# A borrowed PSUM bank for the first product of a quad, in a Mamba-2 plus PReLU kernel

## The chip, the cores and the metric

The kernel runs on one core of one Trainium2 chip. The metric is the device time in microseconds (us), the median of several runs; the time before is 369.48 us (three runs, 368.27 to 370.26). A profile of one execution, with a span of 366.2 us, gives the times of single instructions. Engines are named as the profile names them: PE is TensorE (matmuls; PEld are its weight loads), DVE is VectorE, ACT is ScalarE, POOL is GpSimd, SP issues DMAs.

## The reference, cut to what matters

A chunked state-space scan makes `x` of 3072 tokens by 256 features, and a two-layer network with a PReLU follows:

```python
# scan, per batch and head, in chunks of 32 tokens (the kernel uses chunks of 128)
y_intra = einsum('bhij,bhjd->bhid', (C @ B^T) * L, x)      # L: decays, causal
y_inter = einsum('bhin,bhnd->bhid', C, state) * exp(cum)
state   = decay_full * state + sum_j(B_j x_j * decay_from_j)
# network: 3072 tokens, d_model 256, d_ff 2048
h = x @ w_in
g = maximum(h, 0) + alpha * minimum(h, 0)
out = g @ w_out
```

All of it is in float32. The network's two products are most of the arithmetic.

## The kernel before, the parts concerned

**Seven products in place of eight.** Five of the six groups of 512 tokens go through a Strassen-like scheme on 2x2 blocks. A *quad* is a step of this scheme: (group g, z), four blocks of 128 hidden features, two halves of 256 tokens. There are 4 quads (z = 0 to 3) in each of the groups 1 to 5, so 20 in all. In a quad, seven first products (`first`) fill the hidden blocks. Each has two matmuls of 128x256, and each of these matmuls is two records in the trace, so a `first` is four records. Seven second products (`product`) of the quad before are strewn between them; `after(j)` is the place where they, and the scan's work, are slipped in.

```python
def quad(g, z, after):
    b11, b12, b21, b22 = ...            # blocks of x (transposed); t1..t4 their differences
    A, Y = (ps_h.tile([P, GT], F32, name="hp")... for i in range(2))   # the two "hp" banks

    def first(to, w, b, start=False):
        for p in range(2):
            nc.tensor.matmul(to[:, p], w(2 * z + p), b, start=start and p == 0, stop=True, ...)

    first(A, lambda q: wi[:, q, 0, 0], b11, True)          # M1
    m1 = tile_of(wtp, "m1", "wt")
    nc.scalar.copy(out=m1, in_=A)                          # L823: M1 is kept in SBUF
    after(1)
    first(Y, lambda q: s1[:, q], t1, True)
    m5 = tile_of(wtp, "m5", "wt")
    nc.scalar.copy(out=m5, in_=Y)                          # L827
    after(2)
    after(3)
    first(A, lambda q: s2[:, q], t2)                       # accumulates on M1 in A
    u2 = tile_of(wtp, "u2", "wg")
    nc.scalar.copy(out=u2, in_=A)                          # L832
    after(4)
    nc.vector.tensor_tensor(out=Y, in0=Y, in1=u2, op=ALU.add)      # L834
    after(5)
    first(A, lambda q: wi[:, q, 1, 0], t3)
    nc.vector.tensor_tensor(out=c22, in0=A, in1=m5, op=ALU.add)    # L838
    after(6)
    first(Y, lambda q: s4[:, q], b22)
    prelu(g12, Y, z, 0)                                    # ACT L798, then DVE L800
    prelu(g22, c22, z, 1, (nc.scalar,))
    nc.scalar.copy(out=Y, in_=m1)                          # L844: M1 back into a bank
    prelu(g22, c22, z, 1, (nc.vector,))
    after(7)
    after(8)
    nc.gpsimd.tensor_tensor(out=tc_, in0=g22, in1=g12, op=ALU.subtract)   # L849
    first(A, lambda q: wi[:, q, 1, 1], t4)
    prelu(g21, A, z, 1)
    after(9)
    after(10)
    first(Y, lambda q: wi[:, q, 0, 1], b21)                # M1 + this product
    prelu(g11, Y, z, 0)
    for o, x0, x1 in ((ta, g12, g11), (tb, g22, ta), (td, tb, g21)):
        eng.tensor_tensor(out=o, in0=x0, in1=x1, op=ALU.subtract)         # L858
    ...
    after(11) ... after(14)
```

`product(g, z, n)` (its matmuls are L790) multiplies block n with weights of `w_out` and accumulates in one of four banks; n = 1, 2, 3 use g11, g21, g22, and 4, 5, 6, 7 use td, ta, tb, tc_.

**PSUM.** There are two `ss` banks (pool `ps_s`, 2 buffers), two `hp` banks (pool `ps_h`, 2 buffers), and four held ones (`bank(0)` to `bank(3)`). Outside the start of the kernel, `ss_tile()` takes the next `ss` bank in turn.

**The scan of later pairs of chunks** runs beside the quads, as a generator whose stages are called from `after`. A pair takes two quads: its last stages run in an odd quad (z = 1, 3), its decays and its `gram` in the even quad before (z = 0, 2).

```python
def turn_bc(gp):                       # DVE transpose of B and C of the next pair
    ...
def pair(gp):
    ...
    if fine:                           # all pairs beside quads
        for k in range(2):
            for w in range(2):
                half_decays(k, w)      # two DVE scans, L460
                if k == 1 and w == 1:
                    spread_c()         # ACT L551
                    c_decayed()        # POOL L554
                yield
    ...
    # gram: 8 matmuls into 2 ss banks and 2 hp banks (L605), then 4 DVE multiplies (L639)
    ...
    if fine and gp + 1 < NP:
        turn_bc(gp + 1)
    yield
    ys = [ss_tile() for w in range(KC)]            # y: matmuls L662, L670
    ...
```

Each scan reads `abc`, which a DMA brings (two of 512 KB for a pair). Of a pair's four `half_decays`, one was called at `after(14)` of the odd quad before, and the others at `after(1)`, `after(2)` and `after(5)` of the even quad. The gram is at `after(13)` of the even quad.

```python
with_gram = {5: ((1,), (2, (0,))), 7: ((2, (1,)), (3,)), 8: ((5, (0,)),), 11: ((5, (1,)), (7,)),
             13: ((6,),), 14: ((4,),)}          # even quads of groups 1 to 4
without = {3: ((1,),), 5: ((2,),), 7: ((3,),), 8: ((5,),), 9: ((7,),), 13: ((6,),), 14: ((4,),)}
for i in range(NZ * (NG - 1)):
    g, z = divmod(NZ + i, NZ)
    nxt = 2 * g + 2                             # NP = 12: no pair is left in group 5
    ...
    quad(g, z, after)
close(NG - 1)
```

The instruction order on each engine is that of the program.

Of the kernel before, what the change touches and what calls it, by code (L numbers as in the profile page):

```python
# [9 lines left out]
F32 = mybir.dt.float32  # L10
U32 = mybir.dt.uint32
U16 = mybir.dt.uint16
ALU = mybir.AluOpType
# [9 lines left out]
def kernel(  # L23
# [25 lines left out]
    nc = tc.nc  # L49
# [4 lines left out]
    batch, H, S, D = x.shape  # L54
    N = B.shape[-1]
    P = 128
    Q = 128
# [11 lines left out]
    NP = NCH // 2  # L69
# [15 lines left out]
    wtp = ctx.enter_context(tc.tile_pool(name="wtp", bufs=3))  # L85
    lda = ctx.enter_context(tc.tile_pool(name="lda", bufs=3))
    ldx = ctx.enter_context(tc.tile_pool(name="ldx", bufs=3))
    work = ctx.enter_context(tc.tile_pool(name="work", bufs=2))
# [4 lines left out]
    gp = ctx.enter_context(tc.tile_pool(name="gp", bufs=16))  # L93
# [12 lines left out]
    ident_p = []  # L106
    m5_bank = []

    def ss_tile():
        if early[0] is None:  # L110
            return ps_s.tile([P, 512], F32, name="ss")
        early[0] += 1
        i = early[0] % (3 if ident_p else 4)
        return ps_s.tile([P, 512], F32, name="ss") if i < 2 else bank(i)


    loads = {}
# [158 lines left out]
    def keep_warm(to, n, cols=2 * Q):  # L276

        for i in range(n):
# [8 lines left out]
                          in_=ident.unsqueeze(1).to_broadcast([P, H, Q]))  # L287
# [137 lines left out]
        return ps_h.tile([P, GT], F32, name="hp", tag="hp")  # L425

    bcs = {}

    def turn_bc(gp):

        bcs[gp] = work.tile([P, 4, Q], F32, name="bc")
        nc.vector.transpose(
            bcs[gp].rearrange("p (i k) t -> p i (k t)", i=2)
            .rearrange("p i (c b) -> p i b c", b=8),
            loads["p", gp][0][:, 1:].rearrange("p e i (b n) -> p (i b) e n", n=N))

    def pair(gp):

        b, c = divmod(2 * gp, CPB)
        nat, abc, xt, ap = loads["p", gp]  # L440
        last = c + 2 == CPB
        fine = gp >= 2 * GC // 2
        dec = work.tile([P, 2, H, Q], F32, name="dec")
        dv = dec.rearrange("p k h t -> p k (h t)")

        def decays(k):

# [7 lines left out]
                                             initial=0.0, op0=ALU.mult, op1=ALU.add)  # L455

        def half_decays(k, w):
            for i in range(2):
                hs = slice((2 * w + i) * 2 * Q, (2 * w + i + 1) * 2 * Q)
                nc.vector.tensor_tensor_scan(out=dv[:, k, hs], data0=abc[k][:, hs],  # L460
                                             data1=ident_p[0], initial=0.0, op0=ALU.mult,
                                             op1=ALU.add)

        ahead = {}

# [1 line left out]
        if gp == 0:  # L467
            z = first_a(ap, nc.vector)
# [105 lines left out]
        if fine:  # L574
            for k in range(2):
                for w in range(2):
                    half_decays(k, w)
                    if k == 1 and w == 1:
                        spread_c()
                        c_decayed()  # L580
                    yield
        else:
            if gp > 1:
                states(added(ss_tile()))
                c_decayed()
            decays(0)
            if gp == 1:
                dps = added(dps)
            if gp:
                yield  # L590
            if gp != 1:
                decays(1)
            if gp > 1:
                spread_c()
# [199 lines left out]
    def prelu(o, h, z, i, by=(nc.scalar, nc.vector)):  # L794

        fs = [slice(4 * z + 2 * p + i, 4 * z + 2 * p + i + 1) for p in range(2)]
        for p in range(2 if nc.scalar in by else 0):
            nc.scalar.mul(o[:, p], h[:, p], s_alpha[:, fs[p]])  # L798
        for p in range(2 if nc.vector in by else 0):
            nc.vector.scalar_tensor_tensor(out=o[:, p], in0=h[:, p], scalar=s_mul[:, fs[p]],  # L800
                                           in1=o[:, p], op0=ALU.mult, op1=ALU.max)

    def quad(g, z, after):


        b11, b12 = (xts[g][:, 0, h * HT : (h + 1) * HT] for h in range(2))
        b21, b22 = (xts[g][:, 1, h * HT : (h + 1) * HT] for h in range(2))
        t1, t2, t3, t4 = xsums[g]
        s1, s2, s4 = in_sums
        A, Y = (ps_h.tile([P, GT], F32, name="hp").rearrange("p (q t) -> p q t", q=2)  # L810
                for i in range(2))

        def first(to, w, b, start=False):
            for p in range(2):
                nc.tensor.matmul(to[:, p], w(2 * z + p), b, start=start and p == 0, stop=True,  # L815
                                 skip_group_check=True)

        def tile_of(pool, name, tag):
            return pool.tile([P, 2, HT], F32, name=name, tag=tag)

        first(A, lambda q: wi[:, q, 0, 0], b11, True)
        m1 = tile_of(wtp, "m1", "wt")
        nc.scalar.copy(out=m1, in_=A)  # L823
        after(1)
        first(Y, lambda q: s1[:, q], t1, True)
        m5 = tile_of(wtp, "m5", "wt")
# [3 lines that stand above are left out]
        first(A, lambda q: s2[:, q], t2)  # L830
        u2 = tile_of(wtp, "u2", "wg")
        nc.scalar.copy(out=u2, in_=A)  # L832
        after(4)
        nc.vector.tensor_tensor(out=Y, in0=Y, in1=u2, op=ALU.add)  # L834
        after(5)
        first(A, lambda q: wi[:, q, 1, 0], t3)
        c22 = tile_of(wtp, "c22", "wg")
        nc.vector.tensor_tensor(out=c22, in0=A, in1=m5, op=ALU.add)  # L838
        after(6)
        first(Y, lambda q: s4[:, q], b22)  # L840
        g12, g22, g21, g11 = (tile_of(gp, "gt", "gt") for i in range(4))
        prelu(g12, Y, z, 0)
        prelu(g22, c22, z, 1, (nc.scalar,))
        nc.scalar.copy(out=Y, in_=m1)  # L844
        prelu(g22, c22, z, 1, (nc.vector,))
        after(7)
        after(8)
        ta, tb, tc_, td = (tile_of(gp, "gt", "gt") for i in range(4))
        nc.gpsimd.tensor_tensor(out=tc_, in0=g22, in1=g12, op=ALU.subtract)  # L849
        first(A, lambda q: wi[:, q, 1, 1], t4)  # L850
        prelu(g21, A, z, 1)
        after(9)
        after(10)
        first(Y, lambda q: wi[:, q, 0, 1], b21)
        prelu(g11, Y, z, 0)
        for o, x0, x1 in ((ta, g12, g11), (tb, g22, ta), (td, tb, g21)):
            eng = nc.vector if g == NG - 1 and z == NZ - 1 and o is not td else nc.gpsimd
            eng.tensor_tensor(out=o, in0=x0, in1=x1, op=ALU.subtract)  # L858
        blocks[g, z] = {1: g11, 2: g21, 3: g22, 4: td, 5: ta, 6: tb, 7: tc_}
        after(11)  # L860
        after(12)
        after(13)
        after(14)
# [157 lines left out]
    for f in range(FIRST, NF):  # L1021
# [21 lines left out]
        if f in in_steps:  # L1043
# [18 lines left out]
            14: ((2, 1), (3, 1))}  # L1062


    with_gram = {5: ((1,), (2, (0,))), 7: ((2, (1,)), (3,)), 8: ((5, (0,)),), 11: ((5, (1,)), (7,)),
                 13: ((6,),), 14: ((4,),)}
    without = {3: ((1,),), 5: ((2,),), 7: ((3,),), 8: ((5,),), 9: ((7,),), 13: ((6,),), 14: ((4,),)}
    for i in range(NZ * (NG - 1)):
        g, z = divmod(NZ + i, NZ)
        nxt = 2 * g + 2  # L1070

        def after(j, g=g, z=z, i=i, nxt=nxt):
            places = with_gram if nxt < NP and z % 2 == 0 else without
            for n in places.get(j, ()) if i else ():
                product(*divmod(NZ + i - 1, NZ), *n)
            if i == 0:
                for f, half in last_out.get(j, ()):
                    output(NF - LATE + f, half)
            if (i, j) in ((0, 13), (1, 2)):
                store_first(i)  # L1080
            for args in late_sums.get((i, j), ()):
                weight_sums(*args)
            if g > 1 and z == 0 and j in (7, 11, 13, 14):
                if j == 7:
                    comb[0] = combine(g - 1)
                next(comb[0], None)
            if g > 1 and z in (1, 3) and j == 11:
                finish(g - 1, z // 2)
            if nxt + steps.get((z, j), NP) < NP:
                ssm(nxt + steps[z, j])  # L1090

                if j == 5 and z % 2:
                    for p in (1, 0, 1):
                        if nxt + z // 2 + p < NP:
                            ssm(nxt + z // 2 + p)
            if nxt < NP and (z, j) == (3, 7):
                token_sums(g + 1)
            ahead = nxt + {(0, 9): 1, (2, 9): 2}.get((z, j), NP)
            if ahead < NP:
                if ahead == 6:  # L1100
                    rows_turn(1, held["pr"])
                bns[ahead] = pair_loads(ahead)

        comb = [None] if i == 0 else comb
        if z == 0 and nxt < NP:
            load_pair(nxt + 1)
        if z == 2 and nxt + 2 < NP:
            load_pair(nxt + 2)
        quad(g, z, after)
    close(NG - 1)  # L1110


# [28 lines left out]
```

## Time and profile before

| | |
|---|---|
| median time | 369.48 us |
| span of the profiled execution | 366.2 us |
| busy, PE / PEld | 359.1 / 287.8 us |
| busy, DVE / ACT / POOL | 253.1 / 175.6 / 201.7 us |
| granted TensorE clock | 1.00 |
| quads begin / end on PE (first matmul of L815 to the last product) | 81.7 us / 361.5 us |

Read the busy times as shares of the span: only PE is near all of it. But a matmul's time in the trace overlaps the next one's, so a busy PE may still be held up. What tells is the distance between the starts of matmuls that follow each other.

### The profile page before, as it was taken

What the parts mean: (1) busy time and instruction counts of PE and PEld (TensorE: products, weight loads), DVE (VectorE), ACT (ScalarE), POOL (GpSimd) and SP (SyncE); (2) the same over time, 40 slices, a digit from 0 to 9 for tenths busy, and PEclk for the clock granted to TensorE, in tenths of its full rate; (3) what the DMA queues carried; (4) which work ended last, traced back from release to release, by engine and by line L of the source; (5) the groups of instructions that cost most, each with busy time, mean ns of one, the idle gap of its engine ahead of it and who ended that gap; (6) DMA issues with size and microseconds to landing.
All of it is one profiled execution on the core that took longest, in us unless ns stands there. A gap on an engine that the chain in (4) does not pass through costs nothing.

```text
span 366.2 us, 6758 instructions
## 1 busy us (share of the span) xinstructions
PE 359.1 (98%) x2515; PEld 287.8 (79%) x2515; DVE 253.1 (69%) x469; ACT 175.6 (48%) x377; POOL 201.7 (55%) x211
## 2 busy tenths in 40 slices
PE   8989999999999999999999999999999999999996
PEld 8766666568888888788788788788788788888884
DVE  7897999968648848848748858658858634643364
ACT  1657956426355345444444544445445434544441
POOL 4876666779938855725635626537436345254512
PEclk9999999999999999999999999999999999999999
DMA  7989998822075302004503603701711001001004
GB/s 147 199 180 345 239 284 187 178 61 57 30 167 108 100 3 59 0 2 75 154 3 66 163 5 57 173 2 32 166 37 29 2 2 29 1 2 29 0 0 89
DMA packets 111017, 31.68 MB, mean 87 GB/s; under 512 B 79288, under 2 KB 106888, under 8 KB 110984
## 3 DMA queue, kind: packets, MB, share of 16 engines
q1 hardware_dynamic: 105872, 30.66, 35.5%
q10 hardware_dynamic: 5112, 0.59, 1.1%
q8 instruction: 20, 0.33, 0.4%
q14 instruction: 13, 0.11, 0.1%
HBM read 27.89 MB, written 3.34 MB: 85 GB/s over the span
## 4 chain that ended last, share of the span: by engine, by line
PE 83%; DVE 8%; DMA 4%; POOL 2%; issue 1%; ACT 1%; ACTq 0%; POOLq 0%; SPq 0%; DVEq 0%
PE hp L815 35%; PE bank L790 33%; PE bank L729 4%; PE ss L670 3%; DVE dec L460 3%; PE hp L691 2%; PE ss L605 2%; DMA rows<-in_a_dram 2%; PE ss L662 1%; DVE wr L248 1%; DMA nat<-in_B_dram 1%; PE hp L706 1%; DMA raw<-in_moe_w_in_dram 1%; DVE gt L695 1%; DVE wr L247 1%
## 5 line engine op out<-in xcount | busy, mean ns | idle before, releaser
L858 POOL TENSOR_TENSOR gt<-gt 128x512 f32<-128x512 f32 x58 | 73.6, 1270 | 37.4 <-DVE gt L800 30.7
L790 PE MATMUL bank<-gt,w_out 128*128 128x256 f32 x320 | 82.4, 381 | 0.0
L800 DVE SCALAR_TENSOR_TENSOR gt<-hp,s_mul,gt 128x256 f32<-128x256 f32 x120 | 52.4, 479 | 42.3 <-ACT gt L798 40.2
L798 ACT ACTIVATE gt<-hp,s_alpha 128x256 f32<-128x256 f32 x120 | 50.3, 470 | 50.1 <-PE hp L815 42.7
L790 PEld LDWEIGHTS bank<-gt,w_out 128*128 128x128 f32 x320 | 60.1, 190 | 10.4 <-issue 2.3
L790 PE MATMUL bank<-gt,ws 128*128 128x256 f32 x240 | 59.5, 379 | 0.0
L849 POOL TENSOR_TENSOR gt<-gt 128x512 f32<-128x512 f32 x20 | 25.4, 1270 | 56.0 <-DVE gt L800 56.0
L790 PEld LDWEIGHTS bank<-gt,ws 128*128 128x128 f32 x240 | 45.6, 190 | 6.2
L460 DVE TENSOR_TENSOR_SCAN dec<-abc,bank 128x256 f32<-128x256 f32 x80 | 48.0, 659 | 0.0
L815 PE MATMUL hp<-xs,w_in 128*128 128x256 f32 x160 | 42.3, 387 | 0.0
L815 PE MATMUL hp<-xT,w_in 128*128 128x256 f32 x160 | 41.9, 384 | 0.1
L815 PE MATMUL hp<-xs,ws 128*128 128x256 f32 x160 | 40.7, 382 | 0.0
L823 ACT COPY m<-hp 128x512 f32<-128x512 f32 x20 | 11.7, 586 | 52.9 <-PE hp L815 48.1
L815 PEld LDWEIGHTS hp<-xT,w_in 128*128 128x128 f32 x160 | 29.2, 190 | 7.1 <-ACT hp L844 2.9
L815 PEld LDWEIGHTS hp<-xs,ws 128*128 128x128 f32 x160 | 29.8, 190 | 5.5 <-POOL gt L858 1.1
L815 PEld LDWEIGHTS hp<-xs,w_in 128*128 128x128 f32 x160 | 29.3, 190 | 5.6 <-ACT u L832 0.6
L834 DVE TENSOR_TENSOR hp<-hp,u 128x512 f32<-128x512 f32 x20 | 13.8, 690 | 27.3 <-ACT u L832 27.3
L729 PE MATMUL bank<-w_out,gt 128*128 128x256 f32 x128 | 31.0, 384 | 0.0
L729 PEld LDWEIGHTS bank<-w_out,gt 128*128 128x128 f32 x128 | 23.7, 190 | 6.4 <-issue 3.3
L513 POOL TENSOR_TENSOR sm<-state,bmask 128x256 f32<-128x256 f32 (+1 forms) x12 | 7.9, 656 | 31.8 <-DVE state L510 31.7
L691 PE MATMUL hp<-xT,w_in 128*128 128x512 f32 x48 | 22.8, 597 | 0.4 <-DVE gt L718 0.2
L800 DVE SCALAR_TENSOR_TENSOR gt<-c,s_mul,gt 128x256 f32<-128x256 f32 x40 | 21.3, 573 | 0.0
(157 smaller groups left out, 542.5 us busy)
## 6 DMA issues: line engine op xcount, KB each, us to landing
abc<-z SPq DMA_DIRECT2D x20, 512.0 KB
raw<-in_moe_w_in_dram SPq DMA_DIRECT2D x8, 512.0 KB
raw<-in_moe_w_out_dram SPq DMA_DIRECT2D x8, 512.0 KB
xt<-in_x_dram SPq DMA_DIRECT2D x24, 128.0 KB
nat<-in_B_dram SPq DMA_DIRECT2D x36, 64.0 KB
out_dram<-o_sb SPq DMA_DIRECT2D x32, 64.0 KB
nat<-in_C_dram SPq DMA_DIRECT2D x22, 64.0 KB
ap<-pf SPq DMA_DIRECT2D x11, 128.0 KB
```

Source lines behind the costliest of these rows:

```text
L460: nc.vector.tensor_tensor_scan(out=dv[:, k, hs], data0=abc[k][:, hs], data1=ident_p[0], initial=0.0, op0=ALU.mult, op1=ALU.add)
L670: nc.tensor.matmul(y[w][32 * q : 32 * q + 32, k], xt[:, k, h * D : (h + 1) * D], dec[:, k, h], start=False, stop=True, tile_position=(0, 3 ...
L691: nc.tensor.matmul(hp, w_in[:, k, f * P : (f + 1) * P], xts[g][:, k], start=(k == 0), stop=(k == KC - 1))
L729: nc.tensor.matmul(pos[0][t // 2][:, t % 2], gt[:, t * Q : (t + 1) * Q], w_out[:, f], start=(f == 0 and t % 2 == 0), stop=(f == NF - 1), s ...
L790: nc.tensor.matmul(ms[g][i][:, h], w, blocks[g, z][n][:, p], start=(q == 0 and h == 0), stop=(q == NQ - 1), skip_group_check=True)
L798: nc.scalar.mul(o[:, p], h[:, p], s_alpha[:, fs[p]])
L800: nc.vector.scalar_tensor_tensor(out=o[:, p], in0=h[:, p], scalar=s_mul[:, fs[p]], in1=o[:, p], op0=ALU.mult, op1=ALU.max)
L815: nc.tensor.matmul(to[:, p], w(2 * z + p), b, start=start and p == 0, stop=True, skip_group_check=True)
L823: nc.scalar.copy(out=m1, in_=A)
L834: nc.vector.tensor_tensor(out=Y, in0=Y, in1=u2, op=ALU.add)
L849: nc.gpsimd.tensor_tensor(out=tc_, in0=g22, in1=g12, op=ALU.subtract)
L858: eng.tensor_tensor(out=o, in0=x0, in1=x1, op=ALU.subtract)
```

## The change: what it does and what it is for

In 12 of the 20 quads (the even ones of groups 1 to 4, and all four of the last group; `third` is true there) the first product M1 is made in an `ss` bank, Z, in place of A. ACT then copies Z into A, and Z itself stays as it is. So M1 needs no copy in SBUF and no copy back into Y, and the product that is added to it for g11 can be made early, at `after(5)`, in Z. In even quads the second products stand in another order (`with_gram`): half of product 1 comes at `after(3)`, between the copy of Z and the product that needs it, and products 3 and 5 at `after(9)`. The first two scans of a pair are moved from `after(14)` of an odd quad to `after(1)` of that odd quad, right behind the transposes of `turn_bc`; the other stages move up accordingly, so that an even quad has two scans fewer in front of L834. All this is meant to take waits of PE for ACT and DVE out of the even quads.

```diff
+    decs = {}
+    def scan_half(dec, abc, k, w):          # the body of half_decays, moved out
+        ...
     def turn_bc(gp):
         ...
+        decs[gp] = work.tile([P, 2, H, Q], F32, name="dec")
+        scan_half(decs[gp], loads["p", gp][1], 0, 0)
@@ pair
-        dec = work.tile([P, 2, H, Q], F32, name="dec")
+        dec = decs.pop(gp) if gp in decs else work.tile([P, 2, H, Q], F32, name="dec")
+        begun_scans = gp in bcs
@@ pair, if fine
-                    half_decays(k, w)
+                    if begun_scans and (k, w) != (1, 1):
+                        if (k, w) != (1, 0):
+                            half_decays(*divmod(2 * k + w + 1, 2))
+                    else:
+                        half_decays(k, w)
@@ quad
-    def quad(g, z, after):
+    def quad(g, z, after, third):
...
-        first(A, lambda q: wi[:, q, 0, 0], b11, True)
-        m1 = tile_of(wtp, "m1", "wt")
-        nc.scalar.copy(out=m1, in_=A)
+        if third:
+            Z = ss_tile().rearrange("p (q t) -> p q t", q=2)
+            first(Z, lambda q: wi[:, q, 0, 0], b11, True)
+            nc.scalar.copy(out=A, in_=Z)
+        else:
+            (as before)
...
         nc.vector.tensor_tensor(out=Y, in0=Y, in1=u2, op=ALU.add)
+        g12, g22, g21, g11 = (tile_of(gp, "gt", "gt") for i in range(4))
+        if third:
+            first(Z, lambda q: wi[:, q, 0, 1], b21)
+            prelu(g11, Z, z, 0, (nc.scalar,))
         after(5)
         first(A, lambda q: wi[:, q, 1, 0], t3)
         nc.vector.tensor_tensor(out=c22, in0=A, in1=m5, op=ALU.add)
+        if third:
+            prelu(g11, Z, z, 0, (nc.vector,))
         after(6)
...
-        nc.scalar.copy(out=Y, in_=m1)
+        if not third:
+            nc.scalar.copy(out=Y, in_=m1)
...
-        first(Y, lambda q: wi[:, q, 0, 1], b21)
-        prelu(g11, Y, z, 0)
+        if not third:
+            first(Y, lambda q: wi[:, q, 0, 1], b21)
+            prelu(g11, Y, z, 0)
@@ the order of second products
-    with_gram = {5: ((1,), (2, (0,))), 7: ((2, (1,)), (3,)), 8: ((5, (0,)),), 11: ((5, (1,)), (7,)),
-                 13: ((6,),), 14: ((4,),)}
+    with_gram = {3: ((1, (0,)),), 5: ((1, (1,)), (2, (0,))), 7: ((2, (1,)), (3, (0,))),
+                 9: ((3, (1,)), (5,)), 11: ((7,),), 13: ((6,),), 14: ((4,),)}
...
-        quad(g, z, after)
+        quad(g, z, after, nxt >= NP or z % 2 == 0)
```

More of the change, by code (lines that the diff above doesn't have):

```diff
@@ L427 @@
     bcs = {}
+    decs = {}
+    def scan_half(dec, abc, k, w):
+        dv = dec.rearrange("p k h t -> p k (h t)")
+        for i in range(2):
+            hs = slice((2 * w + i) * 2 * Q, (2 * w + i + 1) * 2 * Q)
+            nc.vector.tensor_tensor_scan(out=dv[:, k, hs], data0=abc[k][:, hs],
+                                         data1=ident_p[0], initial=0.0, op0=ALU.mult,
+                                         op1=ALU.add)
     def turn_bc(gp):
@@ L457, in half_decays @@
         def half_decays(k, w):
[L458 to L462, printed above, removed]
+            scan_half(dec, abc, k, w)
         ahead = {}
@@ L819, in tile_of @@
             return pool.tile([P, 2, HT], F32, name=name, tag=tag)
-        first(A, lambda q: wi[:, q, 0, 0], b11, True)
-        m1 = tile_of(wtp, "m1", "wt")
-        nc.scalar.copy(out=m1, in_=A)
+        if third:
[3 more added lines that the diff above has]
+        else:
+            first(A, lambda q: wi[:, q, 0, 0], b11, True)
+            m1 = tile_of(wtp, "m1", "wt")
+            nc.scalar.copy(out=m1, in_=A)
         after(1)
@@ L838, in quad @@
         nc.vector.tensor_tensor(out=c22, in0=A, in1=m5, op=ALU.add)
+        if third:
+            prelu(g11, Z, z, 0, (nc.vector,))
         after(6)
         first(Y, lambda q: s4[:, q], b22)
-        g12, g22, g21, g11 = (tile_of(gp, "gt", "gt") for i in range(4))
         prelu(g12, Y, z, 0)
         prelu(g22, c22, z, 1, (nc.scalar,))
-        nc.scalar.copy(out=Y, in_=m1)
+        if not third:
+            nc.scalar.copy(out=Y, in_=m1)
         prelu(g22, c22, z, 1, (nc.vector,))
```

## The prediction

> **What bounds the kernel now.** I read the page first: the busy times, then the chain of work that ended last.
>
> ```profile
> span 366.2 us, 6758 instructions
> PE 359.1 (98%) x2515; PEld 287.8 (79%) x2515; DVE 253.1 (69%) x469; ACT 175.6 (48%) x377; POOL 201.7 (55%) x211
> ...
> PE 83%; DVE 8%; DMA 4%; POOL 2%; issue 1%; ACT 1%; ACTq 0%; POOLq 0%; SPq 0%; DVEq 0%
> ```
>
> PE is the bound, and the change takes no matmul away. So it can only bring what PE loses between matmuls. That isn't in the busy share, so I took the timeline of PE and subtracted starts. The last group, where no scan runs, gives the unit (columns: start, us, engine, line, operation, tiles, count):
>
> ```profile
> 344.13 1.03 PE L815 MATMUL hp<-xs,ws 128*128 128x256 f32 x4
> 345.00 1.03 PE L790 MATMUL bank<-gt,w_out 128*128 128x256 f32 x4
> 345.86 1.03 PE L815 MATMUL hp<-xs,ws 128*128 128x256 f32 x4
> 346.73 1.03 PE L790 MATMUL bank<-gt,w_out 128*128 128x256 f32 x4
> ```
>
> The reader is to see that four records start 0.864 us after the four before, whatever a record's length says. A quad has 14 such groups, 12.10 us; in the last group quads begin 12.16 to 12.23 apart. So there is next to nothing to win there. An even quad of group 3 (194.80 to 208.82, 14.02 us) looks otherwise:
>
> ```profile
> 195.62 3.54 DVE L460 TENSOR_TENSOR_SCAN dec<-abc,bank 128x256 f32<-128x256 f32 x6
> 195.66 2.03 PE L815 MATMUL hp<-xs,ws 128*128 128x256 f32 x8
> 195.86 0.58 ACT L823 COPY m<-hp 128x512 f32<-128x512 f32 x1 [1.69 <-PE hp L815]
> ...
> 197.53 1.46 PE L790 MATMUL bank<-gt,w_out 128*128 128x256 f32 x6
> ...
> 198.82 1.03 PE L815 MATMUL hp<-xs,w_in 128*128 128x256 f32 x4
> 199.08 0.67 DVE L834 TENSOR_TENSOR hp<-hp,u 128x512 f32<-128x512 f32 x1
> 199.81 0.73 PEld L815 LDWEIGHTS hp<-xT,ws 128*128 128x128 f32 x4 [0.36 <-DVE hp L834]
> 199.81 1.13 PE L815 MATMUL hp<-xT,ws 128*128 128x256 f32 x4
> ...
> 200.78 0.59 PE L790 MATMUL bank<-gt,w_out 128*128 128x256 f32 x2
> ...
> 202.50 1.03 PE L815 MATMUL hp<-xs,w_in 128*128 128x256 f32 x4
> 202.92 0.59 ACT L844 COPY hp<-m 128x512 f32<-128x512 f32 x1 [0.26 <-DVE gt L800]
> 203.56 0.73 PEld L815 LDWEIGHTS hp<-xT,w_in 128*128 128x128 f32 x4 [0.43 <-ACT hp L844]
> 203.56 1.13 PE L815 MATMUL hp<-xT,w_in 128*128 128x256 f32 x4
> 204.53 0.59 PE L790 MATMUL bank<-gt,ws 128*128 128x256 f32 x2
> ```
>
> Three waits stand in it. First, the group at 195.66 takes 1.87 in place of 1.73: the third product accumulates in A and waits until L823 has copied A (ends 196.44), 0.14. Second, 198.82 to 199.81 is 0.99, not 0.86: Y isn't ready, since L834 came behind six scans (3.54 us) on DVE, 0.13; and the group after a wait takes 0.97, so restarting costs 0.10 more. Third, 202.50 to 203.56 is 1.06: PE waits for the copy L844 of M1 back into Y, 0.20, and 0.10 for the restart. The sum is 0.67.
>
> **What the Trainium skill says.** "Perfetto Trace Analysis", Identifying the Most-Contended Engine, says that matmul busy time is no measure of how near PE is to its limit, because pipelined instructions look smaller than they are; the trace agrees: 98% busy, with the waits above inside it. Its Optimization Strategy says that the same gap repeated on the engine that should be full can mean that there are too few buffers in SBUF or PSUM; the third wait is of this kind, as M1 leaves its bank only because A and Y are the sole two. "TensorE: Matmul & The Clock Gate", Step-by-step, says that the drain of one matmul lies under the filling of the next, and that a matmul by itself can't hide it; the 0.10 per restart agrees in kind. "ScalarE: Activation LUTs", in its own Step-by-step, holds that ACT writes faster to PSUM than to SBUF; the trace shows no such gain: L844 into PSUM 0.59, L823 out of PSUM 0.58. For the new copy, PSUM to PSUM, I take 0.6.
>
> **The change part by part.** The same subtraction over all eight even quads of groups 1 to 4 gives, in order, 0.19, 0.14, 0.44, 0.61, 0.67, 0.61, 0.66 and 0.61, together 3.93 us. Their lengths after group 1 are 13.80 to 14.02; without the waits each would be 13.36. The gaps of about 0.3 before and behind the gram and the y matmuls I leave out: the change doesn't touch them.
>
> Now an even quad after the change, from its first matmul at 0, by these durations. Z takes 0 to 0.86, Y to 1.73, half of product 1 to 2.16. ACT starts 0.2 after Z's end (195.66 to 195.86) and is done at 1.66, so the third product starts at 2.16 without a wait: the 0.14 goes. It ends at 3.02, the g11 product in Z at 3.89, 2 half products at 4.75. The copy u2 is done at 3.8; DVE has four scans in front instead of six (2.4 us; begun some 0.8 in, as before, done at 3.2), so L834 ends at 4.5. PE needs Y at 5.62: 1.1 to spare, the second wait goes. L844 is gone, and with it the third. Next A: c22 follows two scans and the end of the t3 product (5.62 plus 0.2), and ends near 6.5; PE wants A again at 7.34, 0.8 to spare. The g11 prelu is 0.84 on ACT and 0.88 on DVE, the same work at another place; ACT has a copy (0.59) less. DVE ends g21 at about 10.5 with the sums of the group before; the gram needs A and Y at 11.2. So all three waits go: 3.93.
>
> Against this, the very first quad: its Z takes the `ss` bank whose last readers are the two state updates on DVE, which end at 81.92, where the first matmul now starts at 81.68. I put +0.35 there.
>
> In the last group, each quad loses 0.08 at the t3 product, which waits for u2; with the g11 product in between it is covered: 4 x 0.08 = 0.3. The tail is a row of products without gaps from 353.7 to 361.5 and then the last store; g11 comes earlier, but nothing there waits for it by more than 0.1.
>
> The moved scans: two of them (1.25) now stand in front of L834 in odd quads. DVE idles 1.6 to 2.9 us there before L834, in the quads that also combine a group's sums 0.95, so there L834 ends 0.3 later (near 214.1 in place of 213.8 in group 3). PE needs Y only behind the y matmuls at about 216.0. No loss.
>
> Sum: 3.93 - 0.35 + 0.3 = 3.9. In an in-order program with this many crossings I expect a rest to show up again, some 0.4. So 3.5 of 369.48: 366.0 us.
>
> **The rivals.** *DVE takes over the wait in even quads.* The g11 prelu now lies between c22 and g12, where before DVE had a gap; the slack at A is 0.8 and at the gram 0.7, both from my own adding up. If either fails, each even quad gets a new wait of 0.2 to 0.4 and a restart of 0.1: 7 times 0.4 is 2.8, and the time is about 368.7. For it speaks that DVE is busy 12.2 of the 14.0 us in this quad; against it, that an even quad loses two scans.
>
> *The moved scans meet an unfinished load.* The `abc` of the next pair is issued at 204.3 in this window and the trace's DMA packets for it end at 211; the scans would start at 212.15, on the earlier of the two halves. At least 1 us to spare, and another 2 before PE feels it. In the even quads with z = 2 the bytes end at 238.3, the scans start near 239.5. If it went wrong it would cost under 1 us in each of seven odd quads, up to 372.
>
> *The borrowed bank holds up the gram or y.* Z is free when DVE ends g11, near 7.3, and the gram wants both `ss` banks at 11.2. 3.9 us to spare; I give this little.
>
> *Nothing gained.* The waits removed could come back at the next crossing, as PE is in order and a faster quad reaches POOL's differences (3.97 us from 195.16) sooner. But their first reader, product 5, is at 8.6 into the quad. 369, unlikely.
>
> **Range and chances.** If all goes as walked through, the time is 365.5; if half is given back, 367.5; the runs before spread by 1 us to either side. So 364.9 to 367.9 for eight in ten. More than 2% faster (below 362.1) would need more than all PE loses in quads: 0.03. Slower by over 2% needs a new wait of 0.6 in each of 12 quads: 0.02. Within 2%: 0.95.
>
> **What would show it.** On PE's timeline even quads of groups 2 to 4 last 13.3 to 13.5 us; no idle of PEld at the first matmul of t3, s4, t4 or the Z product; no L844 there in the list of waits. The first quad shows a wait for the state update. Odd quads keep their length. I am wrong if even quads stay at 13.8 or more, with PEld idle before the t4 product or the gram and DVE named as the releaser, or if odd quads grow, with DVE idle before the moved scans.

## The result, and the profile after

The changed kernel takes 364.24 us (median of four runs, 363.33 to 364.62) against 369.16 of the kernel before in the same series (368.27 to 370.26). The ratio is 0.9862, with a 95% interval of 0.9828 to 0.9896: 4.9 us less, where 3.5 were predicted, and below the low end of the range (364.9). It is within 2%.

The page of the profile after, the lines that answer to those of before:

```profile
span 362.8 us, 6733 instructions
...
PE 353.6 (97%) x2515; PEld 288.7 (80%) x2515; DVE 250.5 (69%) x469; ACT 168.9 (47%) x365; POOL 201.5 (56%) x211
```

The reader is to see that the number of matmuls and DVE instructions is the same, and that ACT has 12 instructions less: the 12 quads with the borrowed bank save one copy each. The spans differ by only 3.4. That is because the start of the kernel, which the change doesn't touch, varies from run to run: its end (the first matmul of L497 in the first quad's scan, L505 after) lies at 80.82 in the profile before, at 82.06 in the one after, and between 80.4 and 82.5 over all runs below; and from the last matmul to the end of the span it is 0.4 more in the profile after. So I compare in between. Two distances on PE serve for everything that follows:

- the *stretch*: from the first to the last quad's second first product (the `s1` product): 261.59 before, 256.24 after, -5.35;
- the *whole*: from that L497 matmul to the last matmul of the kernel: 281.86 before, 276.84 after, -5.02. This agrees with the medians (-4.92). It differs from the stretch because the first quad's wait (0.46, below) lies ahead of the stretch, and 0.13 gained at the very end lies behind it.

The even quad of group 3 that the prediction showed, in the timeline after (start, us, engine, line, operation, tiles, count):

```profile
194.82 2.38 DVE L434 TENSOR_TENSOR_SCAN dec<-abc,bank 128x256 f32<-128x256 f32 x4
194.86 1.03 PE L827 MATMUL hp<-xs,ws 128*128 128x256 f32 x4
...
195.06 0.57 ACT L838 COPY hp<-ss 128x512 f32<-128x512 f32 x1 [1.69 <-PE ss L827]
...
195.72 0.59 PE L802 MATMUL bank<-gt,w_out 128*128 128x256 f32 x2
...
196.15 1.03 PE L827 MATMUL hp<-xs,ws 128*128 128x256 f32 x4
...
197.01 1.03 PE L827 MATMUL ss<-xT,w_in 128*128 128x256 f32 x4
...
197.88 1.03 PE L802 MATMUL bank<-gt,w_out 128*128 128x256 f32 x4
197.89 0.70 DVE L853 TENSOR_TENSOR hp<-hp,u 128x512 f32<-128x512 f32 x1 [0.69 <-ACT u L851]
...
198.74 1.03 PE L827 MATMUL hp<-xs,w_in 128*128 128x256 f32 x4
...
199.60 1.03 PE L827 MATMUL hp<-xT,ws 128*128 128x256 f32 x4
...
200.47 0.59 PE L802 MATMUL bank<-gt,w_out 128*128 128x256 f32 x2
...
200.90 0.59 PE L802 MATMUL bank<-gt,ws 128*128 128x256 f32 x2
...
201.33 1.03 PE L827 MATMUL hp<-xs,w_in 128*128 128x256 f32 x4
```

Every group of four records now starts 0.86 to 0.87 after the one before it, and every group of two 0.43. All three waits are gone. DVE, which had made PE wait for L834, itself waits 0.69 for ACT before L853. The quad lasts 13.36, as the prediction had it without waits. The list of what PE waited for, over all first products (L827) of the kernel after (us, times):

```profile
its engine sat idle before it (us, times) until:
  PE ss L544: 0.4, 1
  DVE state L518: 0.2, 1
  issue: 0.2, 1
```

The first two entries are one wait, that of the first quad's Z (at 83.27 and 83.30). The third stands behind the y matmuls of an odd quad (295.48) and names no other engine.

Where the 5.35 comes from, by quads (from one quad's second first product to the next one's; us):

| quads | before | after |
|---|---|---|
| first (group 1, z = 0) | 15.16 | 14.39 |
| third (group 1, z = 2) | 14.16 | 13.48 |
| six even quads of groups 2 to 4 | 13.81, 13.97, 14.03, 13.97, 14.03, 13.98 | 13.36 each |
| eight odd quads | 13.89 to 14.12 | the same |
| last group, three distances | 12.23, 12.17, 12.17 | 12.09 each |

Taken from unrounded times, the six even quads give 3.60, the last group 0.30. The two even quads of group 1 give 0.77 and 0.68, which is 1.45; the prediction had 0.33 for them.

### The profile page after: what moved, and what is told of

The parts are those of the page before. It is cut to its first block, busy times and chain, and to the rows that moved or that the text cites. A ratio compares the mean times of both kernels' runs of the same rounds, so it can differ in the third digit from the quotient of the medians.

```text
span 362.8 us, 6733 instructions
## 1 busy us (share of the span) xinstructions
PE 353.6 (97%) x2515; PEld 288.7 (80%) x2515; DVE 250.5 (69%) x469; ACT 168.9 (47%) x365; POOL 201.5 (56%) x211
## 4 chain that ended last, share of the span: by engine, by line
PE 82%; DVE 7%; DMA 5%; SPq 2%; ACT 1%; issue 1%; POOL 0%; POOLq 0%; DVEq 0%; ACTq 0%
PE bank L802 33%; PE hp L827 28%; PE ss L827 6%; PE bank L741 3%; DMA raw<-in_moe_w_in_dram 3%; PE ss L682 2%; PE ss L617 2%; DVE dec L434 2%; DMA rows<-in_a_dram 2%; PE hp L703 1%; PE ss L674 1%; DVE wr L248 1%; DVE dec L466 1%; PE hp L279 1%; SPq L164 1%
## 5 line engine op out<-in xcount | busy, mean ns | idle before, releaser
L802 PE MATMUL bank<-gt,w_out 128*128 128x256 f32 x320 | 83.5, 381 | 0.0
L812 DVE SCALAR_TENSOR_TENSOR gt<-hp,s_mul,gt 128x256 f32<-128x256 f32 x96 | 42.0, 479 | 30.0 <-ACT gt L810 27.8
L810 ACT ACTIVATE gt<-hp,s_alpha 128x256 f32<-128x256 f32 x96 | 40.4, 472 | 39.9 <-PE hp L827 26.2
L827 PE MATMUL hp<-xs,w_in 128*128 128x256 f32 x160 | 41.9, 384 | 0.0
L827 PE MATMUL hp<-xs,ws 128*128 128x256 f32 x160 | 41.1, 379 | 0.0
L853 DVE TENSOR_TENSOR hp<-hp,u 128x512 f32<-128x512 f32 x20 | 13.9, 697 | 28.8 <-ACT u L851 28.8
L827 PEld LDWEIGHTS hp<-xs,ws 128*128 128x128 f32 x160 | 30.4, 190 | 4.1
L827 PEld LDWEIGHTS hp<-xs,w_in 128*128 128x128 f32 x160 | 29.7, 190 | 4.6 <-issue 0.2
L827 PE MATMUL ss<-xT,w_in 128*128 128x256 f32 x96 | 24.7, 380 | 0.2 <-DVE state L518 0.2
L842 ACT COPY m<-hp 128x512 f32<-128x512 f32 x8 | 4.7, 587 | 37.6 <-PE hp L827 37.6
L851 ACT COPY u<-hp 128x512 f32<-128x512 f32 x20 | 11.7, 586 | 20.0 <-PE hp L827 20.0
L827 PE MATMUL hp<-xT,ws 128*128 128x256 f32 x80 | 20.5, 379 | 0.0
```

Of the source, the lines that this page charges most:

```text
L802: nc.tensor.matmul(ms[g][i][:, h], w, blocks[g, z][n][:, p], start=(q == 0 and h == 0), stop=(q == NQ - 1), skip_group_check=True)
```

## The experiments

Theory W is the prediction's: the gain is the sum of PE's waits in even quads. It had to be enlarged by waits in group 1 that the prediction didn't count. Theory W takes any matmul that covers a wait to be as good as another. Rival D holds that DVE is what holds PE up, so that the moved scans bring the gain; rival B, that it is the bank itself, so that little is gained without it. (These letters are not those of the prediction's own rivals.) The change has three parts, so I ran each alone, and the whole without each.

| kernel | median (before in the same series) | ratio, 95% | stretch | whole |
|---|---|---|---|---|
| before | | | 261.59 | 281.86 |
| after | 364.24 (369.16) | 0.986 (0.983 to 0.990) | 256.24 | 276.84 |
| bank alone | 363.49 (368.45) | 0.985 (0.980 to 0.989) | 256.93 | 277.54 |
| order alone | 369.07 (368.45) | 1.000 (0.998 to 1.003) | 261.50 | 281.77 |
| scans alone | 367.31 (368.45) | 0.995 (0.993 to 0.998) | 260.32 | 280.70 |
| scans undone | 363.32 (368.45) | 0.983 (0.979 to 0.987) | 256.24 | 276.84 |
| order undone | 364.39 (369.15) | 0.985 (0.981 to 0.989) | 256.94 | 277.53 |
| bank undone | 367.08 (369.15) | 0.994 (0.992 to 0.996) | 260.00 | 280.40 |
| bank in the last group alone | 368.52 (369.15) | 0.998 (0.997 to 1.000) | 261.30 | 281.69 |
| no bank in group 1 | 364.28 (369.15) | 0.986 (0.982 to 0.990) | 257.67 | 277.81 |
| one more DVE addition | 364.28 (369.06) | 0.988 (0.985 to 0.991) | 257.58 | 278.18 |
| two more DVE additions | 371.15 (369.06) | 1.006 (1.004 to 1.008) | 264.05 | 284.65 |
| first quad's Z covered | 363.03 (369.06) | 0.984 (0.982 to 0.987) | 255.38 | 276.38 |
| the same, scans undone | 362.37 (368.55) | 0.985 (0.982 to 0.987) | 255.37 | 276.38 |

Runs of one kernel differ by 0.3 to 4 us, so differences under 1 us are read from the two distances, not from the medians. Each distance comes from one profile, but they repeat well: the sum of the eight odd quads agrees within 0.003 us over all fourteen profiles, and the first quad, in the kernels without the bank there, within 0.03.

### Each part alone

**The bank alone** (`third` as in the change, old `with_gram`, scans at their old places).

> Borrowed bank in the same 12 quads, old order of second products, old places of the scans. I read the stretch from the first to the last quad's second first product on PE: 261.6 us before, 256.2 us after. Theory W (the gain is the sum of the waits of PE in even quads and behind them at the gram of group 1): the copy of M1 back into Y and the late g11 are gone, the late L834 is covered by the g11 product, only the wait for the first copy (about 0.14 a quad) stays: 256.8 to 257.6. Rival D (DVE is what holds up PE, so the moved scans carry the gain): 259.5 or more, with PE waiting for L834.

Measured: stretch 256.93, so 4.66 of the 5.35. The even quads of groups 2 to 4 last 13.43 or 13.49; what is left of the waits is the first copy, as expected. The timeline of this kernel there (lines of PE, ACT and PEld):

```profile
193.53 2.02 PE L825 MATMUL hp<-xs,ws 128*128 128x256 f32 x8
...
193.73 0.57 ACT L836 COPY hp<-ss 128x512 f32<-128x512 f32 x1 [1.69 <-PE ss L825]
...
194.41 0.73 PEld L825 LDWEIGHTS hp<-xs,ws 128*128 128x128 f32 x4 [0.26 <-POOL gt L882]
...
195.38 1.03 PE L825 MATMUL ss<-xT,w_in 128*128 128x256 f32 x4
```

Eight records take 1.85, not 1.73. PEld names POOL, but the matmul reads no tile that POOL was writing then; the copy into A ends at 194.30, and the load follows at 194.41. Rival D, which had 259.5 or more here, falls.

**The order alone.**

```diff
-        quad(g, z, after, nxt >= NP or z % 2 == 0)
+        quad(g, z, after, False)                        # and decs, begun_scans taken out
```

> Only the new order of second products in even quads of groups 1 to 4; M1 copied out and back as before, scans as before. Theory W with cover as the cause: any half product between a copy and its reader hides it, so the waits for the first copy, for L834 and for the copy back go in seven even quads, the first quad (which has no such products) and the last group keep theirs: 257.8 to 258.8. Rival B (the bank itself is what removes the waits): 260.5 or more, as M1 still goes out and back, and g11, now 1.3 us later in the quad, holds up the gram.

Measured: 261.50, against 257.8 to 258.8 expected, and where rival B had it (260.5 or more). My reading of the order was wrong: by itself it moves waits, it doesn't remove them. The weight loads (PEld) in the timeline of the even quad of group 3, with the order alone:

```profile
198.89 0.73 PEld L825 LDWEIGHTS hp<-xs,w_in 128*128 128x128 f32 x4 [0.28 <-issue]
199.97 0.73 PEld L825 LDWEIGHTS hp<-xT,ws 128*128 128x128 f32 x4 [0.36 <-DVE hp L851]
...
201.78 0.73 PEld L825 LDWEIGHTS hp<-xs,w_in 128*128 128x128 f32 x4 [0.21 <-issue]
```

The wait for the first copy and the one for the copy back are gone, but the half product that was moved to `after(3)` had lain between the u2 copy and the t3 product, which now waits (198.89). L834 (L851 here) is as late as before, and the t4 product now waits too (201.78); besides, the later g11 lengthens the gram: from its first matmul to the next product it takes 1.30 (206.72 to 208.02), before it took 1.07 (206.78 to 207.85). The quad lasts 14.03, as before. The second products that can be strewn in are seven to a quad; here a new order only chose which wait lay bare.

**The scans alone** (old `with_gram`, no bank).

> Only two scans of a pair moved up by a quad. Theory W: only the wait for L834 goes, 0.13 plus 0.10 of restart in five or six even quads: 260.2 to 260.6. Rival D: 258 or less.

Measured: 260.32, -1.27, at the expected size: the wait for L834 goes in five even quads, and the one for the copy back stays (PEld at L827 idles 2.9 us for it, eight times, as before).

### The whole without one part

**Without the moved scans.**

```diff
-        decs[gp] = work.tile([P, 2, H, Q], F32, name="dec")
-        scan_half(decs[gp], loads["p", gp][1], 0, 0)
-        begun_scans = gp in bcs
+        begun_scans = False
```

> The changed kernel with the scans at their old places. Theory W: L834 ends 1.2 us later, near where PE needs Y (5.62 us into the quad, by my walk 5.7): 256.2 to 257.3. Rival D: 258.5 or more.

Measured: 256.24, the same as after to 0.01. So the moved scans, worth 1.27 by themselves, are worth nothing beside the bank; nor with the old order (bank alone 256.93, order undone 256.94). The timeline of the even quad of group 3 without the moved scans (this profile begins it 1.1 us earlier):

```profile
193.74 3.54 DVE L434 TENSOR_TENSOR_SCAN dec<-abc,bank 128x256 f32<-128x256 f32 x6
...
195.94 1.03 PE L825 MATMUL ss<-xT,w_in 128*128 128x256 f32 x4
...
196.80 1.03 PE L800 MATMUL bank<-gt,w_out 128*128 128x256 f32 x4
...
197.20 0.67 DVE L851 TENSOR_TENSOR hp<-hp,u 128x512 f32<-128x512 f32 x1
...
197.66 1.03 PE L825 MATMUL hp<-xs,w_in 128*128 128x256 f32 x4
...
198.53 1.03 PE L825 MATMUL hp<-xT,ws 128*128 128x256 f32 x4
```

There are six scans in front of the addition again and it ends at 197.87; but the g11 product (195.94) has come in between, and PE needs Y only at 198.53. The bank gives PE 0.86 us of work that waits for nothing, just where DVE is late.

**Without the new order.**

> The changed kernel with the old order of second products. Theory W: the half product between Z's copy and the third first product is gone, so about 0.14 a quad is waited for in seven even quads: 257.0 to 257.5 for the stretch that is 256.2 after. If the order matters more than that (rival: late readers of POOL's differences), 258 or more.

Measured: 256.94, +0.70, at the low edge of what was expected (257.0 to 257.5). So the order pays 0.70 beside the bank, where the g11 product takes the place of the half product that the t3 product lost. By itself it paid 0.09.

**Without the bank** (order and scans kept).

> The changed kernel without the borrowed bank: new order, moved scans, M1 out and back. Theory W: the first quad's 0.77 and the last group's 0.3 come back, and some of the late g11 at group 1's second gram: 257.3 to 258.2. Rival B: 260 or more.

Measured: 260.00, so -1.59 in all, and the expected 257.3 to 258.2 falls with the order's. The scans alone give 1.27 of it; with them the order brings 0.32. With this all eight combinations of the three parts have been run. The four with the bank lie at 256.24 to 256.94, the four without it at 260.00 to 261.59. Here and with the order alone rival B was right against theory W, here at the very edge of what it allowed (260 or more): the gain is a sum of PE's waits, as theory W has it, but of the three parts it is the bank that removes most of them.

**The bank in the last group alone.**

> The kernel before with the borrowed bank in the last group alone. Theory W: 0.08 in each of four quads: the stretch is 261.2 to 261.4, the last quads 12.09 apart. Time within 0.3 us of before.

Measured: 261.30, distances of 12.09 there: 0.29, as expected. The median is 0.63 under that of before, where at most 0.3 was expected; the whole shows 0.17.

### What the prediction had missed: group 1

```diff
-        quad(g, z, after, nxt >= NP or z % 2 == 0)
+        quad(g, z, after, nxt >= NP or (z % 2 == 0 and g > 1))
```

> The changed kernel with no borrowed bank in the two even quads of group 1 (the first and the third quad). Theory W, with the waits that the prediction left out (the gram there waited for g11, and the first quad's t3 product for a copy): the first quad is back at 15.1, the third, which keeps the new order, is 13.5 to 14.1 in place of 13.48; the stretch is 256.9 to 257.6, and the first quad's first product no longer waits for the state update (0.2 to 0.3). If the extra gain over my sum came from elsewhere (the scan's start, the loads), the first quad stays at 14.4.

Measured: the stretch is 257.67, +1.43; the first quad is back at 15.15, the third at 14.15, a little above what I expected, since the new order brings the third nothing without the bank. So all of what group 1 gained hangs on the bank. In the whole only 0.97 are lost, for the first quad's matmul no longer waits for the state update. The timeline of the kernel before, in its third quad, shows where the time was (lines of POOL, DVE, PEld and PE):

```profile
118.40 1.26 POOL L758 TENSOR_TENSOR ws<-w_out,ws 128x512 f32<-128x512 f32 x1
118.46 2.89 DVE L800 SCALAR_TENSOR_TENSOR gt<-c,s_mul,gt 128x256 f32<-128x256 f32 x2
...
119.63 1.44 POOL L758 TENSOR_TENSOR w_out<-w_out 128x512 f32<-128x512 f32 x1
...
121.28 1.65 DVE L800 SCALAR_TENSOR_TENSOR gt<-hp,s_mul,gt 128x256 f32<-128x256 f32 x4
...
121.54 1.03 PE L790 MATMUL bank<-gt,ws 128*128 128x256 f32 x4
...
122.97 0.18 PEld L605 LDWEIGHTS hp<-cz,bc 32*128 32x128 f32 x1 [0.18 <-DVE gt L800]
...
124.03 1.13 PE L790 MATMUL bank<-gt,w_out 128*128 128x256 f32 x4
```

and the timeline of the changed kernel at the same place:

```profile
120.22 2.07 DVE L812 SCALAR_TENSOR_TENSOR gt<-c,s_mul,gt 128x256 f32<-128x256 f32 x2
...
122.24 1.03 PE L802 MATMUL bank<-gt,ws 128*128 128x256 f32 x4
...
124.28 1.13 PE L802 MATMUL bank<-gt,w_out 128*128 128x256 f32 x4
```

The two DVE instructions of the g22 prelu take 2.89 us together (0.87 where POOL makes no sums), beside sums of weights that POOL makes, as far as the quads go, only in group 1. g21 and g11 come late, and the gram, which wants the banks A and Y, waits in the middle for them: 2.49 us from the product ahead of the gram to the one behind it (121.54 to 124.03), and 2.04 after the change (122.24 to 124.28). That is 0.45 of this quad's 0.68; 0.14 is the first copy, which the prediction counted, and 0.08 a restart at the g11 product (119.27), which it didn't count. After the change the g22 prelu still takes 2.07 us here (120.22 to 122.29), yet the gram doesn't wait: g11 is done before it.

In the first quad, PE at the t3 product and the weight loads (PEld) of the output products ahead of the gram and behind it, before:

```profile
85.13 1.03 PE L729 MATMUL bank<-w_out,gt 128*128 128x256 f32 x4
86.14 1.10 PE L815 MATMUL hp<-xs,w_in 128*128 128x256 f32 x4
87.08 1.03 PE L815 MATMUL hp<-xT,ws 128*128 128x256 f32 x4
...
91.38 1.70 PEld L729 LDWEIGHTS bank<-w_out,gt 128*128 128x128 f32 x8
...
95.00 1.59 PEld L729 LDWEIGHTS bank<-w_out,gt 128*128 128x128 f32 x8 [0.33 <-issue]
```

and these weight loads after:

```profile
92.66 1.70 PEld L741 LDWEIGHTS bank<-w_out,gt 128*128 128x128 f32 x8
...
95.93 1.59 PEld L741 LDWEIGHTS bank<-w_out,gt 128*128 128x128 f32 x8
```

Across the gram it is 3.62 before and 3.27 after: 0.35 of this quad's 0.77. The rest there is 0.19 for the copy back, which the prediction counted, and 0.23 at the t3 product (85.13 to 87.08 is 1.95 in place of 1.73), which it missed, as its subtraction didn't take in the matmuls of `output` (L729).

### How much room is left

An addition of 128x512 was put in front of c22 in the eight even quads, once and twice; its result is overwritten by c22.

```diff
         c22 = tile_of(wtp, "c22", "wg")
+        for _ in range(n if third and g < NG - 1 else 0):       # n is 1 or 2
+            nc.vector.tensor_tensor(out=c22, in0=ident_h[:, :512], in1=ident_h[:, 512:], op=ALU.add)
```

> The changed kernel with one useless DVE addition of 128x512 (about 0.65) in front of c22 in the eight even quads with the borrowed bank. By my walk there were 0.8 us to spare for A and 0.7 for the gram: nothing changes, 256.2 to 256.5. If the change put DVE at its limit (rival), PE waits at the t4 product: 258 or more.

> The same with two such additions (about 1.3): more than the room. PE waits at the t4 product, some 0.45 plus 0.1 of restart a quad, in eight quads: 260 to 262, DVE c22 named as the releaser.

Measured, one: in groups 2 to 4 the even quads last 13.36 or 13.38, no change, as walked through. But the stretch is 257.58, for group 1 isn't as I had it: the first quad is 14.61 (+0.22), the third 14.54 (+1.06). The addition takes 0.67 in groups 2 to 4 and 1.60 and 1.77 in group 1, again beside POOL's sums. Two: the six quads grow by 0.68 to 0.75 each (some 0.55 was expected), those of group 1 by 1.90 and 1.63; the stretch is 264.05, over the 260 to 262 expected, most of it because of group 1. The t4 product is the one that waits, in the timeline with two more additions:

```profile
205.26 0.69 DVE L864 TENSOR_TENSOR c<-hp,m 128x512 f32<-128x512 f32 x1
...
206.06 0.73 PEld L827 LDWEIGHTS hp<-xs,w_in 128*128 128x128 f32 x4 [0.88 <-issue]
206.09 1.10 PE L827 MATMUL hp<-xs,w_in 128*128 128x256 f32 x4 [0.51 <-DVE c L864]
```

So the room in front of c22 is between 0.67 and 1.4 us in groups 2 to 4. In group 1, where the addition itself takes longer, 1.60 us more cost the first quad 0.22, and 1.77 cost the third 1.06. Rival D describes the kernel with two more additions, not the changed kernel.

### A version that beats both

The first quad's Z takes the bank whose readers are two state updates. One half product of the first group's output is put in front of it, and the others move up one place:

```diff
+        if i == 0:
+            output(NF - LATE, 0)
         quad(g, z, after, nxt >= NP or z % 2 == 0)
-    last_out = {3: ((0, 0),), 5: ((1, 0),), ..., 14: ((2, 1), (3, 1))}
+    last_out = {3: ((1, 0),), 5: ((2, 0),), ..., 13: ((2, 1),), 14: ((3, 1),)}
```

> The changed kernel with one half product of the first group's output put in front of the first quad's first product, the others each one place earlier. Theory W: the wait of Z for the state update (0.2 to 0.3) is filled, all else stays: the stretch is 256.2 plus or minus 0.2, the time 0.2 us under the changed kernel, which is less than runs differ by.

> The changed kernel with the scans at their old places and one half product of the first group's output in front of the first quad's first product: what the parts undone so far leave as needed. Theory W: the moved scans bring nothing where the bank is borrowed, so the quads are as in z_covered: a first quad of 13.5 to 13.6, even quads of 13.36, a stretch of 255.3 to 255.6, a time of 362.5 to 363.5. If the scans matter once the first quad is mended, 256 or more.

Measured: the whole is 276.38 for both, 0.46 under after, where 0.2 was expected. (The stretch, 255.38 where 256.0 to 256.4 was expected, is no measure here: one half product of 0.86 has gone in front of it, which the expectation overlooked.) PE's timeline at the first quad's Z, first of the changed kernel, then with Z covered:

```profile
82.42 0.66 PE L544 MATMUL ss<-ident,nat 128*128 128x128 f32 x4
...
83.30 1.10 PE L827 MATMUL ss<-xT,w_in 128*128 128x256 f32 x4 [0.23 <-DVE state L518]
```

```profile
80.93 0.66 PE L544 MATMUL ss<-ident,nat 128*128 128x128 f32 x4
81.42 1.03 PE L741 MATMUL bank<-w_out,gt 128*128 128x256 f32 x4
82.28 1.03 PE L827 MATMUL ss<-xT,w_in 128*128 128x256 f32 x4
```

From the transposes to the next matmul it is 0.88 in the first, 0.49 in the second. The last kernel does without the moved scans and is as good: 362.37 us, ratio 0.9845 (0.9818 to 0.9872), the lowest median of all; that it beats the changed kernel is shown by the traces (0.46), not by the medians, as the intervals of the ratios overlap.

## Why the prediction was wrong

Point by point, by its own steps:

- *What bounds the kernel, and the three waits of an even quad.* Right. All three are gone after the change, the six even quads of groups 2 to 4 last 13.36 as stated, and they gave 3.60, as the prediction's own six numbers sum to.
- *The sum over the eight even quads, 3.93.* This is the step that failed, in its first two terms, 0.19 and 0.14. They were 0.77 and 0.68, so the sum was 5.05, 1.12 more, all of it from group 1. The prediction said of the gram and y matmuls: "The gaps of about 0.3 before and behind the gram and the y matmuls I leave out: the change doesn't touch them." It doesn't touch those, but inside group 1's two grams lay waits for the late g11 and g21 as well, 0.35 and 0.45, and the change removes these; 0.23 and 0.08 outside the grams were left out too. The gram's length, 1.6 and 1.5 in group 1 against 1.07 in group 3, stood in the timeline before. A subtraction that goes over chosen lines finds no waits in the others.
- *The first quad's Z, +0.35.* Right in kind, a little small: from the L497 matmul to the first quad's second first product it is 1.72 before and 2.18 after, 0.46, and covering it brings 0.46.
- *The last group, 0.3.* Right in kind, a little small: 0.30 within the stretch (0.29 with the bank there alone), and 0.13 more in the last quad and the products behind it.
- *The moved scans.* That they cost odd quads nothing is right (13.89 to 14.12, as before), and the loads were there in time. That they were needed in even quads wasn't asked; they aren't.
- *Sum, less 0.4 for a rest that might show up again.* No such rest came. 5.05 and 0.43 less 0.46 is 5.02, and 5.02 is measured on the whole. The discount of 0.4 and the 1.12 together make the error of 1.5; that the two smaller misses, 0.11 and 0.13, cancel is luck.
- *The prediction's four rivals.* None came true: DVE kept room, the scans met finished loads, the bank didn't hold up the gram. The walk's 0.8 us to spare at A fits the additions (0.67 has room, 1.4 has not), except in group 1.

What the runs leave open: in group 1 several causes of the late g11 lie together (POOL's sums, a sum of weights on DVE before g11 in the first quad); they were not taken apart. That the bank removes the wait is shown, by the run without it there; which of the causes made g11 late is argued from the timeline.

## What to carry to other kernels

Where an in-order engine is full but for short waits, sum the distances of the starts over all its instructions, not over the lines that the change names, and by stage: one stage may hide a wait that the others don't have. Strewing the same independent work in another order mostly moved waits about (0.09 us); a buffer that lets one more piece of work start early removes them, here 4.66 of 5.35 us. And parts of a change don't add up: two scans moved were worth 1.27 us alone and 0.00 beside the bank.

## What the runs showed of the hardware

Where the g22 prelu on DVE, which reads two tensors in SBUF (c22 and gt), met an instruction of POOL, at least one of the two was stretched. In the kernel before, each of its instructions took 1.48 us in place of 0.48 in the third quad, and 0.60 to 1.01 in five other places where it met POOL's sums; in the eighth (135.04) it kept to 0.48, and POOL's next sum took 0.99 in place of 0.73. All 120 prelu instructions with one input in PSUM took about 0.48 throughout. The added 128x512 addition took 0.67 alone and 1.60 and 1.77 beside POOL. The Trainium skill, "SBUF — State Buffer", in "SBUF: two separate sides", says that DVE instructions with two SBUF inputs and GpSimd instructions that read SBUF share a port pair, which one of them locks for its whole length; the durations agree, POOL's own being 1.26 to 1.73 there. And ACT's copy from PSUM to PSUM took 0.570, against 0.586 from PSUM to SBUF in the same profile: the borrowed bank costs ACT nothing. The prediction saw no gain in writing to PSUM, but had compared copies out of different memories; from the same one it is 0.016 us.
